# One layout, planner and schedule change in a planned fp32 kernel: operands at one remainder modulo 512 bytes, w2 sums off the operand ring

## The chip, the cores and the metric

One NeuronCore of a Trainium2 chip runs one launch. The metric is device time in microseconds, the median of repeated runs. In the profile, PE is TensorE's matmuls, PEld its weight loads, DVE VectorE, ACT ScalarE, POOL GpSimd, and SP SyncE, which issues every DMA.

## The reference

```python
xn = layernorm(x)                       # x: 2048 x 512, all float32
# A: linear attention, 32 heads of 16
q, k, v = split(xn @ wqkv)              # wqkv: 512 x 1536
pq, pk = phi(q), phi(k)                 # phi(t) = where(t > 0, t + 1, exp(t)) + 1e-6
o = (pq @ (pk.T @ v)) / (pq . sum(pk) + 1e-6)      # per head
A = o @ wo                              # wo: 512 x 512
# B: MLP, F = 1376
B = relu(xn @ w1 + b1) ** 2 @ w2 + b2
out = x + A + B
```

## The kernel before

**Arithmetic.** Products are made to nearly full fp32 precision from `float32r` parts: each operand is split into a rounded high part and the rest (`split`: a copy on ACT, a subtraction on DVE), and each product takes three matmuls of 128 x 512 (high x high, high x rest, rest x high).

**Stages.** Tokens go in tiles of 128. First all tiles are normalised, transposed (tiles 0 to 7 on TensorE, the rest by DVE behind small DMAs that regroup partitions, `xg<-xp`), projected on the k weights `wk`, and summed into `kx` (`acc<-pk,tok`). Then the four blocks of 512 tokens are handled in two pairs (`for n in range(2)`). A pair has a first phase, where each of NK = 7 pairs of column blocks (NQ = 2 of q, NP = 5 of w1) goes through seven half-size products (a Strassen-Winograd scheme on weights and on tokens, the sums of tokens being T1 to T4), and a second phase, `run_jobs`, where 21 jobs (first pair) or more multiply the activations `s` with rows of w2 or of the attention matrix. In the first pair the second phase is plain; in the second pair it uses the Strassen scheme again and so needs sums of blocks of w2.

**Operands.** Weights are split once, in the first pair, into tiles `ops` of two operands (512 KB), used and copied to DRAM (`spill`, into `wd1`, `wd2`, `wdz`), and later read back (`ops<-wd`). Eight slots D0 to D7 form a ring: `advance` hands a free slot to the next entry of the list `needed`, `used` frees a slot when its operands' matmuls are recorded. The w2 sums (`make_t`, from `raw_t` tiles in the slots x0 and x1) are entries of that list with no keys, two behind each of five steps of the second pair's first phase: they take a ring slot, are made by two additions and a split, and are spilled from it. The parts `s` of the activations rotate through five slots `pair0` to `pair4`.

**Order.** All instructions are recorded as tasks with their predecessors. TensorE's order is that of the code. Up to `nc.fixed` (the first tiles) all engines keep it; beyond, `Program.order` plays the program with costs for each instruction (`cost`), gives each task a due time from TensorE's order, and lets each engine, SP's DMA queue too, take the most urgent ready task, in 60 rounds in which waits of TensorE make the tasks before them more urgent (`press`); the best round is emitted. A new tile of a tag (`Place`) waits for the tasks recorded so far of the last tile there.

**Layout.** A tile gets its address when it is first used in the emitted order, behind those before it in its pool. The low pool holds, in the program as built and in bytes per partition: from address 1152 zb 512, ident 512, eps 64, b1s 64; then tiles of 8192 (B0, A0, xs1 high and rest, A1), four `pair` slots of 4096, less_one 64, the fifth `pair` slot, B1 (8192), the slots D and xs0 (both parts 8192), and zc 64. T1 to T4 lie in B0, B1, A0, A1, `wk` in A0 and A1. Small tiles are padded to 64 bytes. The rest, the raw tiles and `hz` among it, lies in a pool above.

**The second phases.** In the first pair the jobs are four attention products, `add_product(NK - 1, 1)` and the `hz` product, then for the second block four attention products, ten of w2 and the `hz` product; two jobs ahead, `parts_of` splits the next `s`. In the second pair `add_product(NK - 1, 1)` stands behind four of the five jobs of the first group.

Of the kernel before, what the change touches and what calls it, by code (L numbers as in the profile page):

```python
# [7 lines left out]
F32 = mybir.dt.float32  # L8
# [10 lines left out]
class Task:  # L19
    __slots__ = ("engine", "name", "args", "kw", "preds", "succs", "dur", "lag", "lock", "due", "ready", "left", "start", "at",  # L20
                 "index", "size", "cause", "behind")


class Place:
# [6 lines left out]
    def real(self):  # L31
        if self.tile is None:
            n = 1
            for k in self.shape[1:]:
                n *= k
            if n % 16 and self.pool.name.startswith("low"):
                t = self.pool.tile([self.shape[0], n + -n % 16], self.dt, name=self.name, tag=self.tag)[:, :n]
                if len(self.shape) > 2:
                    t = t.rearrange("p (a b) -> p a b", a=self.shape[1])
                self.tile = t  # L40
            else:
                self.tile = self.pool.tile(self.shape, self.dt, name=self.name, tag=self.tag)
        return self.tile
# [39 lines left out]
class Program:  # L83
# [29 lines left out]
    def add(self, engine, name, args, kw):  # L113
        t = Task()
        t.engine, t.name, t.args, t.kw, t.index = engine, name, args, kw, len(self.tasks)
        given = [("out" if k == 0 else "in", a) for k, a in enumerate(args)] + [("out" if k == "out" else "in", a) for k, a in kw.items()]
        given = [(k, a) for k, a in given if isinstance(a, (bass.AP, View))]
        outs, ins = ([self.region(a) for k, a in given if k == kind] for kind in ("out", "in"))
        if name == "matmul" and not kw.get("start"):
            ins = ins + outs  # L120
        outs = [r for r in outs if r[0] != self.apart]
        t.preds = {}
        for regions, write in ((ins, False), (outs, True)):
            for r in regions:
                before = self.seen.get(r[0], [])
                hit = [(o, wrote) for q, o, wrote in before
                       if (write or wrote) and q[0] < r[2] and r[1] < q[1] and q[2] < r[4] and r[3] < q[3]]
                if isinstance(r[0], Place) and r[0].last and not hit:
                    hit = [(o, True) for o in r[0].last.tasks]
                for o, wrote in hit:  # L130
                    if o is not t:
                        t.preds[o.index] = max(t.preds.get(o.index, 0), 1 if wrote else 0)
        for regions, write in ((outs, True), (ins, False)):
            for r in regions:
                old = self.seen.get(r[0], [])
                if write:
                    old = [x for x in old if not (x[1] is not t and r[1] <= x[0][0] and x[0][1] <= r[2] and r[3] <= x[0][2] and x[0][3] <= r[4])]
                self.seen[r[0]] = old + [(r[1:], t, write)]
                if isinstance(r[0], Place) and t not in r[0].tasks[-1:]:
                    r[0].tasks.append(t)  # L140
        self.cost(t, [a for k, a in given if k == "out"][0], [a for k, a in given if k == "in"])
        self.tasks.append(t)

    def cost(self, t, out, ins):
# [10 lines left out]
        if t.engine == "tensor":  # L155
            wide = t.name == "matmul" and ins[0].dtype != F32
            t.dur, t.lag = (0.0135 + n / 2400 if wide else 0.055 + n / 2400), 0.23
        elif t.engine == "scalar":
# [6 lines left out]
        elif t.engine == "gpsimd":  # L165
            t.dur = 0.2 + src * 2.3 / 1000 if t.name == "tensor_tensor" else 0.3
            t.lock = t.name == "tensor_tensor"
        else:
            b = 1
            for s, k in out.ap:  # L170
                b *= k
            run = 1
            for a in (out, *ins):
                d = list(a.ap)
                c = d[-1][1] if d[-1][0] == 1 else 1
                run = min(run, c) if run > 1 else c
            t.size, t.lag = 4 * b, 2.0
            t.dur = 0.43 if out.ap[0][1] == P and run >= 512 else 0.62
            t.size = t.size * max(1.0, (0.009 + run * 4 / 27e3) / (run * 4 / 24e3)) if run > 1 else b * 150
# [4 lines left out]
    def order(self):  # L184
# [3 lines left out]
        for t in ts:  # L188
            t.succs = []
        for t in ts:  # L190
            for p, raw in t.preds.items():
                ts[p].succs.append((t, raw))
        when = 0.0
        for t in ts:
            t.due = 1e9
            if t.engine == "tensor":
                t.due = when
                when += t.dur
        for t in reversed(ts):
            e = t.engine  # L200
            took = t.dur if e != "sync" else 2.0 + t.size / 380e3
            for s, raw in t.succs:
                t.due = min(t.due, s.due - took - (t.lag if raw and s.engine != e else 0))
            t.due = min(t.due, when)
# [26 lines left out]
    def play(self):  # L231
# [18 lines left out]
        while done < len(ts):  # L250
# [27 lines left out]
            if e == "sync":  # L278
                dma = end = max(dma, end) + t.size / 380e3
            done += 1  # L280
# [24 lines left out]
def kernel(  # L305
# [10 lines left out]
):  # L316

# [108 lines left out]

    def both(name, tags, dt=F32R, pool=keep):
# [9 lines left out]
    NK = NQ + NP  # L456
    wd1 = [dram.tile([P, 7, 512], F32, name=f"wd1_{k}") for k in range(NK)]
    wd2 = [dram.tile([P, 8, 512], F32, name=f"wd2_{k}") for k in range(NK)]
    wdz = dram.tile([P, 4, 512], F32, name="wdz")
    wdm = [dram.tile([P, 512], F32, name=f"wdm_{j}") for j in range(NJ)]  # L460
    wos = {}
    ident = keep.tile([P, P], F32, name="ident")
    heads = work.tile([P, P], F32, name="heads", tag="heads")
    b1s = keep.tile([P, NF], F32, name="b1s")
    zb = keep.tile([P, P], F32, name="zb")
    zc = keep.tile([P, 2, NJ], F32, name="zc")
    eps = keep.tile([P, 1], F32, name="eps")

# [59 lines left out]
    def spill(kind, k, i, t):  # L528
        n = t.shape[1]
        nc.sync.dma_start(place_of(kind, k, slice(i, i + n)), f32(t))  # L530
        ready.update((kind, k, i + e) for e in range(n))
# [244 lines left out]

    def place_of(kind, k, i):
        return wdz[:, i] if kind == "z" else (wd1 if kind == "1" else wd2)[k][:, i]

    def load_keys(keys):  # L780

        def make(t):
            (kind, k, i), two_of = keys[0], len(keys) == 2
            if two_of and keys[1] == (kind, k, i + 1):
                nc.sync.dma_start(f32(t), place_of(kind, k, slice(i, i + 2)))
            else:
                for e, key in enumerate(keys):
                    nc.sync.dma_start(f32(t[:, e]), place_of(*key))
        return make

    def advance():

        while needed and free_ops:
# [8 lines left out]
            for e, key in enumerate(keys):  # L802
                loaded.setdefault(key, []).append((t[:, e], holder))
            if not keys:
                free_ops.append(tag)

# [14 lines left out]
    def needed_in(n):  # L821
# [6 lines left out]
        for p in range(NK + 1):  # L828
# [13 lines left out]
            if p < NK:  # L842
# [3 lines left out]
                if f >= 0 and n:  # L846
                    o.append(([("2", f, 2)], None))
                if n and 0 < p <= NP:
                    for e in range(2):
                        o.append(([], make_t(p - 1, e)))  # L850

        def attention(make):
            for j in range(NJ):
                both_of("2", NP + j // 2, 2 * (j % 2), make_2(NP + j // 2, j % 2) if make else None)

        if n == 0:
            attention(True)
            both_of("2", NP - 1, 2, make_2(NP - 1, 1))
            both_of("z", 0, 2, make_z(1))
# [6 lines left out]

        keys = [("2", f, 4) for f in range(NP - 1)] + [("2", NP - 1, 2), ("2", NP - 1, 4)]

# [320 lines left out]

    less_one = keep.tile([P, 1], F32, name="less_one")  # L1190
    nc.gpsimd.memset(less_one, -1.0)
# [80 lines left out]
    for n in range(2):  # L1272
# [19 lines left out]

        if n:
            raw_free[:] = ["x0", "x1"]
            raw_jobs += [raw_2(k, "t") for k in range(NP)]
            fetch_raws()
        banks = [bank(f"b{n}_{k}", loop_tag) for k in range(4)]
# [127 lines left out]
        if n == 0:  # L1425
            jobs = [attention_job(acc, 0, j) for j in range(NJ)]
            jobs.append((None, lambda s: add_product(NK - 1, 1)))
            jobs.append(z_job(acc, 0, True))
# [7 lines left out]
            outs.append(lambda: store(res[t1], t1, 0, 1))  # L1436

            def step(e):
                if e == 10:
# [3 lines left out]
                if e > 1:  # L1443
                    do(columns if columns else sums)

            later_jobs = [attention_job(acc_2, 2, j, j == 0) for j in range(NJ)]
# [8 lines left out]
            def prepare(job):  # L1455
                if job[0] is None:
                    return None
                if len(job) == 3:
                    square(job[0])
                return parts_of("s", job[0])  # L1460

            run_jobs([(j[0], j[1]) if len(j) == 2 else (j[0], True, j[1]) for j in jobs + later_jobs],
                     lambda j: prepare(j), 2, step)
            do(outs, len(outs))
            do(columns, len(columns))
# [40 lines left out]

        jobs.insert(NP - 1, (None, lambda s: add_product(NK - 1, 1)))
        o = {}
# [48 lines left out]
```

## Time and profile before

| | |
|---|---|
| median of 3 runs | 440.11 us (439.18 to 440.42) |
| the profiled execution | 439.19 us, span 437.5 us |
| granted clock of TensorE | 0.988 (mean) |
| PE, DVE, ACT busy in the span | 416.8, 325.7, 256.0 us |
| DMA | 96.19 MB, 220 GB/s on average |
| the chain that ended last | PE 84%, DMA 9%, DVE 3% of the span |

PE rows of the timeline give a start and a modelled length: the length of a row runs past the start of the next, so the pace is read from the starts. All instructions come from one recording helper, so their line is always L293 and groups are told apart by tile names.

### The profile page before, as it was taken

What the parts mean: (1) busy time and instruction counts of PE and PEld (TensorE: products, weight loads), DVE (VectorE), ACT (ScalarE), POOL (GpSimd) and SP (SyncE); (2) the same over time, 40 slices, a digit from 0 to 9 for tenths busy, and PEclk for the clock granted to TensorE, in tenths of its full rate; (3) what the DMA queues carried; (4) which work ended last, traced back from release to release, by engine and by line L of the source; (5) the groups of instructions that cost most, each with busy time, mean ns of one, the idle gap of its engine ahead of it and who ended that gap; (6) DMA issues with size and microseconds to landing.
All of it is one profiled execution on the core that took longest, in us unless ns stands there. A gap on an engine that the chain in (4) does not pass through costs nothing.

```text
span 437.5 us, 5497 instructions
## 1 busy us (share of the span) xinstructions
PE 416.8 (95%) x1808; PEld 335.3 (77%) x1808; DVE 325.7 (74%) x551; ACT 256.0 (59%) x438; POOL 27.4 (6%) x48
## 2 busy tenths in 40 slices
PE   8999859999999999999999999999898999999993
PEld 7788648888888888888878888888676887788882
DVE  5899578888868898999919720998787985466953
ACT  5775355664957888888814220568676784435310
POOL 2242122220000000000000000000000000000000
PEclk9999969999999999999999999999999999999998
DMA  7850753921897669754967997798788889958703
GB/s 237 279 152 1 193 168 96 273 65 49 288 327 285 254 235 326 264 214 181 326 250 181 248 347 258 208 306 264 279 248 279 254 253 233 287 160 230 196 0 97
DMA packets 78273, 96.19 MB, mean 220 GB/s; under 512 B 40003, under 2 KB 51267, under 8 KB 77989
## 3 DMA queue, kind: packets, MB, share of 16 engines
q1 hardware_dynamic: 78244, 95.84, 70.1%
q8 instruction: 14, 0.23, 0.2%
q14 instruction: 15, 0.11, 0.1%
HBM read 59.91 MB, written 33.82 MB: 214 GB/s over the span
## 4 chain that ended last, share of the span: by engine, by line
PE 84%; DMA 9%; DVE 3%; SPq 1%; ACT 1%; issue 0%; POOL 0%; POOLq 0%
PE ps L293 48%; PE acc L293 36%; DMA wd<-ops 4%; DMA ops<-wd 2%; DMA xTd<-t 1%; SPq L293 1%; DMA x<-in_A_x_dram 1%; DVE y L293 1%; DMA xg<-xp 0%; DVE xp L293 0%; DVE ops L293 0%; DVE st L293 0%; DVE res L293 0%; DVE o L293 0%; ACT s L293 0%
## 5 line engine op out<-in xcount | busy, mean ns | idle before, releaser
L293 PE MATMUL ps<-s,ops 128*128 128x512 f32 x390 | 95.2, 394 | 0.0
L293 PEld LDWEIGHTS ps<-s,ops 128*128 128x128 f32 x390 | 72.8, 187 | 18.1 <-ACT s L293 0.6
L293 PE MATMUL acc<-s,ops 128*128 128x512 f32 x300 | 74.5, 394 | 2.2 <-ACT s L293 1.4
L293 PEld LDWEIGHTS acc<-s,ops 128*128 128x128 f32 x300 | 55.9, 187 | 16.9 <-ACT s L293 2.3
L293 PE MATMUL acc<-pk,tok 128*128 128x512 f32 x192 | 47.6, 396 | 0.0
L293 ACT ACTIVATE s<-rr 128x512 fp32r<-128x512 f32 x46 | 28.5, 629 | 26.0 <-PE acc L293 13.8
L293 DVE TENSOR_TENSOR s<-rr,s 128x512 fp32r<-128x512 f32 x46 | 31.4, 687 | 16.4 <-ACT s L293 15.3
L293 PE MATMUL ps<-T,ops 128*128 128x512 f32 x168 | 42.4, 394 | 0.0
L293 PEld LDWEIGHTS acc<-pk,tok 128*128 128x128 f32 x192 | 35.7, 189 | 8.4 <-DVE pk L293 0.6
L293 PE MATMUL acc<-T,ops 128*128 128x512 f32 x168 | 42.1, 394 | 0.0
L293 PEld LDWEIGHTS acc<-T,ops 128*128 128x128 f32 x168 | 31.5, 187 | 7.5
L293 PEld LDWEIGHTS ps<-T,ops 128*128 128x128 f32 x168 | 31.4, 187 | 7.4
L293 ACT ACTIVATE rr<-acc 128x512 f32<-128x512 f32 x23 | 13.5, 587 | 20.3 <-PE acc L293 20.1
L293 POOL TENSOR_TENSOR tok<-xp,tok 128x512 fp32r<-128x512 f32 x16 | 22.2, 1390 | 43.4 <-ACT tok L293 38.6
L293 PE MATMUL ps<-xs0h,ops 128*128 128x512 f32 x72 | 23.8, 391 | 0.0
L293 PE MATMUL acc<-xs0h,ops 128*128 128x512 f32 x56 | 18.6, 393 | 3.3 <-DMA ops<-wd 3.3
L293 ACT ACTIVATE ops<-raw 128x512 fp32r<-128x512 f32 (+1 forms) x28 | 16.3, 590 | 7.4 <-DMA raw<-in_B_w_dram 3.2
L293 DVE TENSOR_TENSOR ops<-raw,ops 128x512 fp32r<-128x512 f32 (+1 forms) x28 | 17.0, 618 | 3.5 <-ACT ops L293 3.5
L293 PE MATMUL ps<-wkh,xs1h 128*128 128x512 f32 x32 | 13.5, 433 | 6.3 <-ACT xs1h L293 6.2
L293 DVE TENSOR_TENSOR rr<-acc,rr 128x512 f32<-128x512 f32 x21 | 14.4, 688 | 5.6 <-PE acc L293 4.7
L293 ACT ACTIVATE k<-ps 128x512 f32<-128x512 f32 x16 | 9.5, 594 | 15.2 <-PE ps L293 15.0
L293 ACT ACTIVATE tok<-xp 128x512 fp32r<-128x512 f32 x16 | 10.0, 625 | 10.6 <-POOL xp L293 8.8
(153 smaller groups left out, 735.8 us busy)
## 6 DMA issues: line engine op xcount, KB each, us to landing
wd<-ops SPq DMA_DIRECT2D x45, 512.0 KB, 5.1
ops<-wd SPq DMA_DIRECT2D x43, 512.0 KB, 5.5
ops<-wd SPq DMA_DIRECT2D x42, 256.0 KB, 4.5
res<-in_A_x_dram SPq DMA_DIRECT2D x32, 128.0 KB, 5.3
out_dram<-res SPq DMA_DIRECT2D x32, 128.0 KB, 4.3
x<-in_A_x_dram SPq DMA_DIRECT2D x5, 512.0 KB, 6.3
raw<-in_B_w_dram SPq DMA_DIRECT2D x10, 256.0 KB, 6.5
raw<-in_B_w_dram SPq DMA_DIRECT2D x5, 512.0 KB, 4.7
```

The source lines that it names most:

```text
L293: getattr(getattr(self.nc, t.engine), t.name)(*map(real, t.args), **{k: real(a) for k, a in t.kw.items()})
```

## The change

- `eps`, `b1s`, `zc` and `less_one` become slices of one tile `odds` of 256 bytes; the padding to 64 bytes goes.
- `add` notes the last tile of a place (`first`) and `order` binds a new tile to all its tasks, also those recorded later; due times are worked out in topological order. Costs: matmuls of plain fp32 dearer, DMAs above 64 KB with 2.8 us to land instead of 2.0, 320 GB/s instead of 380.
- `wd1`, `wd2`, `wdz` are laid out by pairs of operands: `[4, P, 2, 512]` instead of `[P, 7 or 8, 512]`.
- The w2 sums leave `needed`: they are made in the first pair's second phase, from the fifth job on, in the slots rp0 and rp1, two a job, once all raw slots are free; spilled from there.
- `add_product(NK - 1, 1)` comes one job earlier in both second phases, and its operand with it in the lists of keys.

```diff
-                    hit = [(o, True) for o in r[0].last.tasks]
+                    t.first.append(r[0].last)
...
-            t.dur, t.lag = (0.0135 + n / 2400 if wide else 0.055 + n / 2400), 0.23
+            t.dur, t.lag = (0.0135 + n / 2400 if wide else 0.055 + n / 2400 if t.name == "transpose" else 0.11 + n / 1200), 0.23
...
-            t.size, t.lag = 4 * b, 2.0
+            t.size, t.lag = 4 * b, 2.8 if b > P * P else 2.0
...
+            for place in t.first:
+                for o in place.tasks:
+                    t.preds.setdefault(o.index, 1)
...
-            took = t.dur if e != "sync" else 2.0 + t.size / 380e3
+            took = t.dur if e != "sync" else t.lag + t.size / 320e3
...
-                dma = end = max(dma, end) + t.size / 380e3
+                dma = end = max(dma, end) + t.size / 320e3
...
-    wd1 = [dram.tile([P, 7, 512], F32, name=f"wd1_{k}") for k in range(NK)]
-    wd2 = [dram.tile([P, 8, 512], F32, name=f"wd2_{k}") for k in range(NK)]
-    wdz = dram.tile([P, 4, 512], F32, name="wdz")
+    wd1 = [dram.tile([4, P, 2, 512], F32, name=f"wd1_{k}") for k in range(NK)]
+    wd2 = [dram.tile([4, P, 2, 512], F32, name=f"wd2_{k}") for k in range(NK)]
+    wdz = dram.tile([2, P, 2, 512], F32, name="wdz")
...
-    b1s = keep.tile([P, NF], F32, name="b1s")
+    odds = keep.tile([P, P // 2], F32, name="odds")
+    b1s, zc = odds[:, 16:16 + NF], odds[:, 32:32 + 2 * NJ].rearrange("p (u j) -> p u j", u=2)
-    zc = keep.tile([P, 2, NJ], F32, name="zc")
-    eps = keep.tile([P, 1], F32, name="eps")
+    eps = odds[:, :1]
...
-                if n and 0 < p <= NP:
-                    for e in range(2):
-                        o.append(([], make_t(p - 1, e)))
...
             for j in range(NJ):
+                if make and j == NJ - 1:
+                    both_of("2", NP - 1, 2, make_2(NP - 1, 1))
                 both_of("2", NP + j // 2, 2 * (j % 2), make_2(NP + j // 2, j % 2) if make else None)
...
-        keys = [("2", f, 4) for f in range(NP - 1)] + [("2", NP - 1, 2), ("2", NP - 1, 4)]
+        keys = [("2", f, 4) for f in range(NP)]
+        keys.insert(NP - 2, ("2", NP - 1, 2))
...
-    less_one = keep.tile([P, 1], F32, name="less_one")
+    less_one = odds[:, 1:2]
...
-        if n:
-            raw_free[:] = ["x0", "x1"]
-            raw_jobs += [raw_2(k, "t") for k in range(NP)]
-            fetch_raws()
...
-            jobs.append((None, lambda s: add_product(NK - 1, 1)))
+            jobs.insert(NJ - 1, (None, lambda s: add_product(NK - 1, 1)))
...
+                if e > 3:
+                    if not made_t and sorted(raw_free) == ["rp0", "rp1", "x0", "x1"]:
+                        raw_free[:] = ["x0", "x1"]
+                        raw_jobs.extend(raw_2(k, "t") for k in range(NP))
+                        fetch_raws()
+                    if len(raw_free) < 4:
+                        for u in range(2 * (len(made_t) < NP)):
+                            make_t(len(made_t), u)(work.tile([P, 2, 512], F32R, name="made", tag=f"rp{u}"))
+                        made_t.append(e)
...
-        jobs.insert(NP - 1, (None, lambda s: add_product(NK - 1, 1)))
+        jobs.insert(NP - 2, (None, lambda s: add_product(NK - 1, 1)))
```

More of the change, by code (lines that the diff above doesn't have):

```diff
@@ L20 @@
     __slots__ = ("engine", "name", "args", "kw", "preds", "succs", "dur", "lag", "lock", "due", "ready", "left", "start", "at",
-                 "index", "size", "cause", "behind")
+                 "index", "size", "cause", "behind", "first")
 class Place:
@@ L32, in real @@
         if self.tile is None:
[L33 to L42, printed above, removed]
+            self.tile = self.pool.tile(self.shape, self.dt, name=self.name, tag=self.tag)
         return self.tile
@@ L121, in add @@
         outs = [r for r in outs if r[0] != self.apart]
-        t.preds = {}
+        t.preds, t.first = {}, []
         for regions, write in ((ins, False), (outs, True)):
@@ L190, in order @@
         for t in ts:
+            for place in t.first:
+                for o in place.tasks:
+                    t.preds.setdefault(o.index, 1)
+            t.left = len(t.preds)
+        for t in ts:
             for p, raw in t.preds.items():
                 ts[p].succs.append((t, raw))
+        line = [t for t in ts if not t.left]
+        for t in line:
+            for s, raw in t.succs:
+                s.left -= 1
+                if not s.left:
+                    line.append(s)
         when = 0.0
@@ L198, in order @@
                 when += t.dur
-        for t in reversed(ts):
+        for t in reversed(line):
             e = t.engine
-            took = t.dur if e != "sync" else 2.0 + t.size / 380e3
+            took = t.dur if e != "sync" else t.lag + t.size / 320e3
             for s, raw in t.succs:
@@ L529, in spill @@
         n = t.shape[1]
-        nc.sync.dma_start(place_of(kind, k, slice(i, i + n)), f32(t))
+        nc.sync.dma_start(place_of(kind, k, i, n), f32(t))
         ready.update((kind, k, i + e) for e in range(n))
@@ L775, with place_of @@
     ready, loaded, owner, needed, free_ops = set(), {}, [], [], []
-    def place_of(kind, k, i):
-        return wdz[:, i] if kind == "z" else (wd1 if kind == "1" else wd2)[k][:, i]
+    def place_of(kind, k, i, n=1):
+        at = slice(i % 2, i % 2 + n)
+        return (wdz if kind == "z" else (wd1 if kind == "1" else wd2)[k])[i // 2, :, at]
     def load_keys(keys):
@@ L784, in make @@
             if two_of and keys[1] == (kind, k, i + 1):
-                nc.sync.dma_start(f32(t), place_of(kind, k, slice(i, i + 2)))
+                nc.sync.dma_start(f32(t), place_of(kind, k, i, 2))
             else:
                 for e, key in enumerate(keys):
-                    nc.sync.dma_start(f32(t[:, e]), place_of(*key))
+                    nc.sync.dma_start(f32(t[:, e:e + 1]), place_of(*key))
         return make
@@ L803, in advance @@
                 loaded.setdefault(key, []).append((t[:, e], holder))
-            if not keys:
-                free_ops.append(tag)
     def op(*key):
@@ L857, in needed_in @@
             attention(True)
-            both_of("2", NP - 1, 2, make_2(NP - 1, 1))
             both_of("z", 0, 2, make_z(1))
@@ L1436 @@
             outs.append(lambda: store(res[t1], t1, 0, 1))
+            made_t = []
             def step(e):
@@ L1463 @@
                      lambda j: prepare(j), 2, step)
+            assert len(made_t) >= NP, made_t
             do(outs, len(outs))
```

## The prediction

> **What bounds the kernel now.** I read the page first, then the stages, then who ended TensorE's waits, and last the start times of single matmuls.
>
> ```profile
> span 437.5 us, 5497 instructions
> PE 416.8 (95%) x1808; PEld 335.3 (77%) x1808; DVE 325.7 (74%) x551; ACT 256.0 (59%) x438; POOL 27.4 (6%) x48
> GB/s 237 279 152 1 193 168 96 273 65 49 288 327 285 254 235 326 264 214 181 326 250 181 248 347 258 208 306 264 279 248 279 254 253 233 287 160 230 196 0 97
> ```
>
> TensorE is busy 95% of the span, so time can come from two places alone: the 20.7 us in which it is idle, and the pace of its matmuls. The stages from 59 us on (projections, first pair's first and second phase, second pair's first and second phase with the tail) give the idle part.
>
> ```profile
> 59.00:107.00 48.00, 47.55 (x195) 38.63 (x196) 41.45 (x59) 30.01 (x50) 10.58 (x12) 0.94 0.47 136
> 107.00:215.00 108.00, 108.00 (x484) 88.01 (x484) 94.53 (x161) 88.15 (x147) 0.52 (x1) 1.00 0.74 261
> 215.00:275.00 60.00, 59.28 (x256) 47.46 (x255) 27.97 (x40) 15.29 (x24) 0.00 (x0) 1.00 0.84 257
> 275.00:365.00 90.00, 85.94 (x369) 68.28 (x368) 77.80 (x133) 64.94 (x106) 0.00 (x0) 1.00 0.87 265
> 365.00:437.50 72.50, 64.60 (x276) 51.33 (x276) 40.40 (x62) 23.14 (x39) 0.00 (x0) 0.97 0.60 167
> ```
>
> The columns are the length, the busy time of PE, PEld, DVE, ACT and POOL, the granted clock, the DMA share and GB/s. From 107 us on TensorE lacks 0.7 us in the first pair's second phase and 4.1 us in the second pair's first phase. The tail's idle time is outside the change. The waits by who ended them:
>
> ```profile
> PE ps L293 <- ACT xs1h L293: 6.2, 1, 6.2
> PE acc L293 <- DMA ops<-wd: 3.3, 2, 1.9
> PE acc L293 <- ACT s L293: 1.4, 2, 0.7
> PE acc L293 <- ACT rr L293: 0.8, 1, 0.8
> ```
>
> 3.3 us are operand loads that came late, 1.4 us are two waits for a moving operand `s`, 0.8 us is the last relu of the second pair, and 6.2 us lie in the start. Now the pace. In the timeline of TensorE, the distance between two rows' starts over the number of matmuls is the pace:
>
> ```profile
> 70.42 2.88 PE L293 MATMUL acc<-pk,tok 128*128 128x512 f32 x12
> 73.14 0.39 PE L293 MATMUL ps<-wkh,xs1h 128*128 128x512 f32 x1
> ...
> 321.88 0.39 PE L293 MATMUL acc<-xs0h,ops 128*128 128x512 f32 x1
> ...
> 324.62 1.56 PE L293 MATMUL acc<-T,ops 128*128 128x512 f32 x6
> 326.02 1.54 PE L293 MATMUL ps<-s,ops 128*128 128x512 f32 x6
> 327.40 0.86 PE L293 MATMUL acc<-T,ops 128*128 128x512 f32 x3
> ```
>
> Equal matmuls run at two paces: `acc<-pk,tok` 2.72/12 = 226.7 ns, `xs0` against `ops` (321.88 to 324.62) 2.74/12 = 228.3 ns, `T` against `ops` 1.40/6 = 233.3 ns, and this `s` 1.38/6 = 230 ns. What tells them apart is where the tiles lie. Adding up the tile sizes in order of first use (the layout above), `ops` and `xs0` start at 320 modulo 512 bytes; `xs1`, T1, T3, T4 and four of the five `pair` slots at 256; T2 and the fifth slot at 320. `pk` and `tok` at 70 us are both at 256. So equal remainders of the moving tile and the weights go with 226.7 ns, after a few irregular matmuls behind each switch (hence 228.3), and a 64-byte difference with 233.3. A long stretch agrees:
>
> ```profile
> 232.07 41.82 PE ps L293 x180
> ```
>
> 41.82/180 = 232.3 ns, which is four fifths of 233.3 and one fifth of 228.3: the mixture of pair slots.
>
> **The change part by part.** *Operands equal modulo 512.* In the new layout only zb and ident (512 bytes each) and `odds` (256) stand ahead of the operands, and all else there is a multiple of 4096: every operand of the low pool gets the same remainder. The groups that leave the slow pace:
>
> ```profile
> L293 PE MATMUL ps<-s,ops 128*128 128x512 f32 x390 | 95.2, 394 | 0.0
> L293 PE MATMUL acc<-s,ops 128*128 128x512 f32 x300 | 74.5, 394 | 2.2 <-ACT s L293 1.4 <-ACT rr L293 0.8
> L293 PE MATMUL ps<-T,ops 128*128 128x512 f32 x168 | 42.4, 394 | 0.0
> L293 PE MATMUL acc<-T,ops 128*128 128x512 f32 x168 | 42.1, 394 | 0.0
> L293 PE MATMUL ps<-xs1h,ops 128*128 128x512 f32 x44 | 15.3, 394 | 0.0
> L293 PE MATMUL acc<-xs1h,ops 128*128 128x512 f32 x28 | 9.9, 394 | 0.0
> L293 PE MATMUL ps<-xs1l,ops 128*128 128x512 f32 x22 | 8.7, 394 | 0.0
> L293 PE MATMUL acc<-xs1l,ops 128*128 128x512 f32 x14 | 5.5, 394 | 0.0
> ```
>
> (390 + 300) x 4/5 + (168 + 168) x 3/4 + 108 = 912 matmuls by 6.67 ns = 6.1 us. The other 138 + 84 of `s` and `T`, some 18 runs of 12, no longer settle anew: 18 x 0.02 = 0.4 us. Sum -6.5 us. The bounds are 0, if the remainders are not the cause, and -7.8 if each of the 195 matmuls of the second stage gained 6.67 ns as well. I take -6.5, since the two paces stand side by side in the rows. It counts in full only while TensorE stays the bound: in the first phase of the first pair DVE works 94.5 of 108 us, and after this step of some 105; in the second pair's 77.8 of 90. Neither becomes the longer one.
>
> By the Trainium skill, "SBUF — State Buffer", section "SBUF: two separate sides", only the port pair that VectorE and GpSimd share causes contention and TensorE never waits on anyone, so addresses could not matter. The two paces of equal matmuls side by side do not agree with that; it is a rival below.
>
> *The sums leave the operand ring.* In the second pair's first phase the ring of eight also carries ten tiles of w2 sums, each holding its slot until its copy to DRAM has landed. The chain of waits passes there:
>
> ```profile
> 297.92 6.67 DMA wd<-ops
> 304.65 4.35 DMA ops<-wd
> 309.14 4.38 PE acc L293 x18
> ```
>
> A copy of 6.67 us frees a slot, the load into it takes 4.35, and TensorE starts 1.9 us late; the second such wait brings it to 3.3. Without these tiles in the ring no load stands behind a copy, and eight slots are ahead of TensorE. -3.3 us; bounds 0 and -3.3. What is late next there is DVE, which loses work as well.
>
> The moved work: eight of the ten sum pairs run after 275 us now (DVE busy, count, clock, DMA share, GB/s of the additions alone):
>
> ```profile
> 231.00:253.00 22.00, 1.60 (x4) 1.00 0.94 232
> 253.00:275.00 22.00, 0.00 (x0) 1.00 0.83 283
> 275.00:297.00 22.00, 2.46 (x6) 1.00 0.92 279
> 297.00:319.00 22.00, 2.35 (x6) 1.00 0.81 263
> 319.00:341.00 22.00, 1.59 (x4) 1.00 0.83 269
> ```
>
> Each is two additions of 0.4 us (6.4 us for sixteen), a rounding copy on ACT and a subtraction on DVE:
>
> ```profile
> 295.36 0.68 ACT L293 ACTIVATE ops<-t 128x512 fp32r<-128x512 f32 x1
> 296.79 0.68 DVE L293 TENSOR_TENSOR ops<-t,ops 128x512 fp32r<-128x512 f32 x1
> ```
>
> So 6.4 + 8 x 0.68 = 11.8 us of DVE and 5.4 us of ACT enter the stage from 215 to 275, where DVE is busy 28 of 60 us and ACT 15: nothing on the path, taken at 0; without that cover it would be 11.8 us. Their DMAs go past SP's queue: at most ten copies and five loads of 512 KB, 7.9 MB. The added waits are those of the copies for DVE; behind them in SP's order stand the operand loads of TensorE. Bounds 0 and the price of the second rival; I take 0, as these bytes are wanted only in the last phase and the loads have eight slots of 12 matmuls (2.75 us each) in hand.
>
> *The product moved one job ahead.* Both waits for `s` have one pattern:
>
> ```profile
> 228.32 0.63 ACT L293 ACTIVATE s<-hz 128x512 fp32r<-128x512 f32 x1 [9.56 <-PE acc L293]
> 229.01 3.06 PE L293 MATMUL acc<-s,ops 128*128 128x512 f32 x12 [0.72 <-ACT s L293]
> ...
> 372.85 1.67 PE L293 MATMUL acc<-s,ops 128*128 128x512 f32 x6 [0.72 <-ACT s L293]
> ```
>
> `add_product(NK - 1, 1)` still uses its pair slot when the job after it, five pairs on, wants the slot: ACT starts when the product ends, TensorE waits 0.72 us. One job earlier, 12 matmuls (6 in the second pair) lie between, 2.7 or 1.4 us against the 0.72 needed. -1.4 us; bounds 0 and -1.4. Its own operand is wanted a job earlier too, which the key lists follow.
>
> *DRAM by operand* changes addresses and no sizes. No row shows the new form; the loads stay eight slots ahead, so 0, and with that cover gone a few tenths either way. *The planner* (late uses, dearer plain fp32 matmuls, slower DMA) keeps TensorE's order but may reorder DVE, ACT, POOL and SP everywhere; no row shows the new order. It could at best take the 6.2 us wait of the start and what the lower clock behind it costs (0.06 of 48 us, 2.9 us), and at worst add a wait of that size: -9.1 to +9.1. I take 0: the edits touch no step of that chain.
>
> Sum: -6.5 - 3.3 - 1.4 = -11.2 us. The profiled execution took 439.19 us, 1.7 of them outside the span, giving 428.0; the median of the runs is 440.11, 0.9 above it, so 428.9.
>
> **The rivals.** *The pace is not set by addresses* (the rule above): only the waits go, 4.7 us, 435.4. Against it: the match at 232.07. For it: only these remainders were seen, not the new one (384). *The first pair's second phase becomes DMA-bound, slower than before.* From 231 to 275 DMA moves (232 + 283) x 22 = 11.3 MB. With 7.9 MB more it has 19.2 MB, and if SP puts them ahead of operand loads, at 283 GB/s that takes 68 us instead of 44: +24 against -11.2, 452.9. It decides from 11.2 us, that is 19.2 MB in 55.2 us, 348 GB/s, about the page's best slice (347). Against it: some of the loads are there already, and nothing asks for the copies before the last phase, so most may flow past 275 us, where the same bytes vanish. Milder, it costs 2 to 6 us. *The plan does not follow*: the sums are off the ring, but the new order opens a wait in the start as large as the present one: +6.2, 435.1. *The plan closes the start's wait*: -9.1, 419.8.
>
> **How the numbers follow.** Forecast as summed 0.68, itself 424 to 433; pace unchanged 0.10; DMA-bound 0.11, half of it beyond the old time; a new wait 0.06; a better start 0.05. 0.3% of 440 us is 1.3 us, about what can be told from no change. Faster 0.90: all but the worse half of the second rival and the tails of the first and third; same 0.03, slower 0.07. The range from 421.5 to 436 takes in the first and third rival and the mild second, and leaves out some 0.15.
>
> **What would show it.** Right: chain rows of 12 matmuls at 2.72 us in all phases and `PE ps x180` near 40.8; no `PE acc <- DMA ops<-wd` row; no 0.72 waits on `ACT s`; additions on `raw_t` all before about 280 us. Wrong: 2.80 rows remaining (pace), `DMA ops<-wd` waits between 215 and 275 us (second rival), a wait on `xs1h` over 6.2 us (third).

## The result and the profile after

The changed kernel takes 415.74 us (median of 4 runs, 415.53 to 416.01); the kernel before 439.64 us (4 runs, 437.17 to 440.42). The ratio is 0.9466 [0.9427, 0.9505], 23.9 us less. The forecast was 428.9 us, its range 421.5 to 436.0: the direction was right, the gain more than twice as large as the 11.2 us forecast.

The page after, its span, the engines and the chain of work that ended last:

```profile
span 414.0 us, 5503 instructions
PE 404.5 (98%) x1808; PEld 334.2 (81%) x1808; DVE 326.8 (79%) x551; ACT 256.4 (62%) x438; POOL 27.8 (7%) x48
PE 96%; DVE 2%; DMA 1%; ACT 0%; issue 0%
```

TensorE was idle for 20.7 us of its span and is idle for 9.5 now; it is also busy 12.3 us less (416.8 to 404.5), with the same 1808 matmuls. The chain is TensorE's almost alone (96%, before 84%): after the first microseconds no DMA stands on it. The stages of the changed kernel (length, busy time of PE, PEld, DVE, ACT and POOL, granted clock, DMA share, GB/s), cut at the same times as before:

```profile
0.00:59.00 59.00, 57.30 (x264) 47.18 (x265) 50.73 (x116) 40.16 (x85) 17.92 (x37) 1.00 0.60 180
59.00:107.00 48.00, 48.00 (x214) 39.74 (x213) 43.10 (x58) 31.33 (x53) 9.33 (x10) 1.00 0.58 175
...
215.00:275.00 60.00, 60.00 (x266) 49.71 (x265) 35.94 (x62) 19.29 (x32) 0.00 (x0) 1.00 0.98 303
275.00:365.00 90.00, 89.22 (x393) 73.32 (x393) 67.47 (x110) 61.88 (x103) 0.00 (x0) 1.00 0.83 244
```

In the second row 214 matmuls are done where it was 195, at a clock of 1.00 where it was 0.94: the start, where the forecast expected nothing, has changed. The 0.94 was a mean. In the kernel before, the clock granted behind the wait on `xs1h` was 0.50 up to 65 us and 1.00 from there:

```profile
59.00:65.00 6.00, 5.55 (x13) 4.39 (x14) 5.89 (x13) 3.61 (x8) 2.02 (x2) 0.50 0.62 208
65.00:107.00 42.00, 42.00 (x183) 34.24 (x183) 35.55 (x47) 26.40 (x43) 8.55 (x10) 1.00 0.45 126
```

What TensorE of the changed kernel still waits for, by who ended the wait:

```profile
PE ps L295 <- DVE odds L295: 1.1, 1, 1.1
PE acc L295 <- ACT rr L295: 0.8, 1, 0.8
PE acc L295 <- DVE xp L295: 0.3, 1, 0.3
PE acc L295 <- DVE y L295: 0.3, 1, 0.3
```

The rows for `xs1h` (6.2 us), for operands from DRAM (3.3 us) and for `s` (1.4 us) are all gone. The pace, in the chain of waits:

```profile
47.01 2.72 PE ps L295 x12
49.73 2.72 PE acc L295 x12
...
218.09 40.80 PE ps L295 x180
```

40.80/180 = 226.7 ns, where the same 180 took 41.82 us.

**Where the 23.5 us of span went.** TensorE's order is that of the code in both kernels, so the start of the n-th matmul in one trace can be set against the n-th in the other. The changed kernel gets ahead by 0.6 us up to 44 us; by 9.3 us between 44 and 65 us of the time before, nearly all of it the wait on `xs1h` (6.4 from start to start, of which 6.2 idle) and the slow matmuls behind it (2.7); by 3.8 us at the two waits for operands and by 2.0 us at the two waits for `s`, each counted from the matmul before the wait to the fourth behind it; and by 7.6 us spread over all other stretches from 65 us on (0.7 up to 107 us, 2.0 up to 215 us, 4.9 after), which is the pace. The last 0.2 us lie behind the last matmul. The 0.6 us of the first 44 are mostly pace too: in the run below that has the new layout alone, the same matmuls are 0.5 us ahead of the kernel before. The forecast had the waits for operands, those for `s` and the pace; the 9.3 us are what it missed.

The missed piece can be read in SyncE's queue. The timeline of its DMA issues in the kernel before (start, length, target and source, count):

```profile
43.06 0.37 SPq L293 DMA_DIRECT2D wv<-in_A_wqkv_dram  x1
43.52 0.52 SPq L293 DMA_DIRECT2D xTd<-t  x1
44.09 12.04 SPq L293 DMA_DIRECT2D xg<-xp  x16
```

its longest wait there (us in total, times, longest):

```profile
SPq L293 <- DVE xp L293: 13.1, 1, 13.1
```

and the same queue in the changed kernel:

```profile
35.35 10.09 SPq L295 DMA_DIRECT2D xg<-xp  x16
45.54 0.57 SPq L295 DMA_DIRECT2D xTd<-t  x1
46.22 1.25 SPq L295 DMA_DIRECT2D wv<-in_A_wqkv_dram  x1
```

The load of `wv` goes into the place of raw tokens (tiles 4 to 7), so it may only start when the last of them has been normalised. These normalisations are recorded behind the first use of `wv`'s place, so the old planner didn't count them: it took the load for ready and put it ahead of the 16 small DMAs `xg<-xp` that regroup tile 8. The queue is worked in order; SyncE stood 13.1 us before the load, and the regrouping of the tile that gives `xs1` waited behind it without need. Now the 16 stand ahead and begin 8.7 us earlier.

### The profile page after: what moved, and what is told of

Same layout as the page of the kernel before. It is cut to its first block, busy times and chain, and to the rows that moved or that the text cites. A ratio compares the mean times of both kernels' runs of the same rounds, so it can differ in the third digit from the quotient of the medians.

```text
span 414.0 us, 5503 instructions
## 1 busy us (share of the span) xinstructions
PE 404.5 (98%) x1808; PEld 334.2 (81%) x1808; DVE 326.8 (79%) x551; ACT 256.4 (62%) x438; POOL 27.8 (7%) x48
## 4 chain that ended last, share of the span: by engine, by line
PE 96%; DVE 2%; DMA 1%; ACT 0%; issue 0%
PE ps L295 51%; PE acc L295 45%; DMA x<-in_A_x_dram 1%; DVE res L295 0%; DVE o L295 0%; DVE st L295 0%; DVE xp L295 0%; DVE y L295 0%; ACT rr L295 0%; DVE mv L295 0%
## 5 line engine op out<-in xcount | busy, mean ns | idle before, releaser
L295 PE MATMUL ps<-s,ops 128*128 128x512 f32 x390 | 92.9, 389 | 0.0
L295 PE MATMUL acc<-s,ops 128*128 128x512 f32 x300 | 72.7, 390 | 0.8 <-ACT rr L295 0.8
L295 PEld LDWEIGHTS acc<-s,ops 128*128 128x128 f32 x300 | 56.2, 188 | 13.1 <-ACT rr L295 1.2
L295 PE MATMUL ps<-T,ops 128*128 128x512 f32 x168 | 41.4, 390 | 0.0
L295 PE MATMUL acc<-T,ops 128*128 128x512 f32 x168 | 41.2, 389 | 0.0
L295 DVE TENSOR_TENSOR ops<-raw,ops 128x512 fp32r<-128x512 f32 (+1 forms) x28 | 18.7, 676 | 1.5 <-ACT ops L295 1.3
L295 ACT ACTIVATE s<-rf 128x512 fp32r<-128x512 f32 x10 | 6.3, 633 | 18.0 <-PE ps L295 17.6
L295 ACT ACTIVATE rr<-rr,odds 128x512 f32<-128x512 f32 x15 | 10.8, 723 | 9.2 <-DVE rr L295 9.1
```

What stands on the lines that cost most here:

```text
L295: getattr(getattr(self.nc, t.engine), t.name)(*map(real, t.args), **{k: real(a) for k, a in t.kw.items()})
```

## The experiments

**One part at a time, on the kernel before.** First the late uses, counted for the one place `wv`:

```diff
...
-                    hit = [(o, True) for o in r[0].last.tasks]
+                    if r[0].name == "wv":
+                        t.first.append(r[0].last)
+                    else:
+                        hit = [(o, True) for o in r[0].last.tasks]
...
```

> The kernel before, with the late uses counted for one place alone, the tile wv of the v weights. Theory (head of line): in the kernel before, the planner believes that the load of wv may start early, because the last readers of the tile that lies there (the normalisations of tokens 4 to 7) are recorded after wv; in truth SP waits for them 13.1 us and the 16 regrouping DMAs of tile 8 stand behind it. With the uses counted the load is put behind these DMAs: the wait on xs1h of 6.2 us and the low clock after it are gone, 439.6 - 9.3 = 430.3 us. Rival (costs): the new DMA and matmul costs of the planner closed the wait; then 439.6 us and the wait of 6.2 us stays.

Measured 429.88 us against 438.71, ratio 0.9797 [0.9768, 0.9826]. Its waits of TensorE:

```profile
PE acc L307 <- DMA ops<-wd: 3.1, 2, 1.7
PE acc L307 <- ACT s L307: 1.4, 2, 0.7
PE ps L307 <- DVE eps L307: 1.1, 1, 1.1
```

No row for `xs1h` is left, the others are those of before, and the 16 `xg<-xp` begin at 37.41 us with the load of `wv` behind them. One load put in the right place of a queue is worth 8.8 us: the missed piece, alone.

Then the layout: `odds` in place of the small tiles, no padding, all else as before.

> The kernel before with the tile odds alone: every operand at 384 modulo 512 bytes, all instructions in the same order. Theory (equal remainders): rows of 12 matmuls take 2.72 us in all phases; 7.0 to 7.5 us less, 432.4 us, with the 6.2 us wait of the start and the late operand loads still there. Rival (addresses do not matter): 439.6 us, PE ps x180 at 41.8 us.

431.71 us, ratio 0.9834 [0.9813, 0.9855], 7.0 us less; the wait on `xs1h` (6.6 us) and that for operands (3.1 us) stay. The 180 matmuls that took 41.82 us take

```profile
227.52 40.80 PE ps L284 x180
```

So addresses alone, with the same instructions in the same order, are worth about what the forecast gave the pace.

The product and its operand one job ahead:

> The kernel before with add_product(NK - 1, 1) one job earlier in both second phases, and its operand with it. Theory (pair slot): the two waits of 0.72 us on ACT s go, with the irregular matmuls behind them 1.8 to 2.0 us, 437.7 us. Rival: the wait comes back elsewhere (on the operand or on the next s), 439.6 us.

436.74 us, ratio 0.9950 [0.9935, 0.9965]: 2.0 us less. Both waits on `s` are gone and the other long waits are as before.

The w2 sums off the ring and into the first pair's second phase:

> The kernel before with the w2 sums made in the first pair's second phase off the operand ring, nothing else. Theory (ring): the two waits of together 3.3 us for ops<-wd in the second pair's first phase go, 3.3 to 3.9 us less, 436.0 us; DVE takes the sums in the stage from 215 to 275 us without a wait of TensorE. Rival (DMA-bound): the copies and loads make operand loads late between 215 and 275 us, waits of 2 us or more there, 438 us or above.

A miss: 455.71 us, ratio 1.0385 [1.0355, 1.0415], 17 us slower. Its waits:

```profile
PE ps L293 <- DMA ops<-wd: 15.8, 3, 14.7
PE acc L293 <- DVE pk L293: 7.8, 1, 7.8
```

The two waits in the second pair went as expected, but at 258 us TensorE began a wait of 14.7 us for an operand, in the phase that the sums were moved into. The second row is the start's wait, which here ends on another tile. Late operands in that phase are what the forecast's second rival had said, and only the rest of the change can have kept them away. Two guesses followed: the planner's dearer DMAs, and the late uses.

> The kernel before with the w2 sums off the ring and the planner's new costs. Made because the sums alone were 17 us slower: TensorE waited 14.7 us for an operand load at 258 us, behind which SP's queue held copies of the tiles made that waited for DVE again and again. Theory (DMA price): with 2.0 us to land the planner took the round trip of a slot rp0 or rp1 (copy out, next sum) for shorter than the 5 to 6 us it takes and issued copies ahead of urgent loads; with 2.8 us and 320 GB/s the wait of 14.7 us is gone and that of 6.2 us in the start stays: 436 us. Rival (late uses): the wait stays, 450 us or more.

455.82 us, ratio 1.0367 [1.0328, 1.0405]: the theory of the prices fell, with the same longest wait of 14.7 us.

> The kernel before with the w2 sums off the ring and all late uses counted, with the old costs. Theory (DMA price): the start's wait goes (9.3 us less), but operand loads are late between 230 and 290 us as with the sums alone: 440 to 446 us. Rival (late uses closed both): no wait in that stage, 426 us.

440.69 us, ratio 1.002 [0.9993, 1.0047]. This lies within what the fallen theory had expected and far above the 426 of its rival. The start's wait is gone, which by the first run is worth 8.8 us, but between 225 and 290 us stand 5.6 us on `s` and 4.5 us on operands. The late uses change the harm and don't end it. Of what is left, the layout of the copies in DRAM is the suspect. In the program, what an access in DRAM touches is one range of addresses:

```python
        reach = sum((n - 1) * s for s, n in dims[1:]) + 1
...
        if not in_psum(a):
            reach += (dims[0][1] - 1) * dims[0][0]
            return a.tensor.name, 0, 1, a.offset, a.offset + reach
```

In a tile `[P, 8, 512]` a pair of operands is strided over all partitions, so its range takes in nearly all of the tile, and the load of one pair counts as dependent on the copy of another that was recorded earlier. Recorded in the first pair's second phase, the copies of the sums come ahead of loads of the same `wd2` tiles; in `[4, P, 2, 512]` each pair has a range of its own.

**The DRAM layout, added and taken away.** Sums off the ring plus the DRAM copies by operand, on the kernel before:

> The kernel before with the w2 sums off the ring and the DRAM copies by operand; planner, layout and job order as before. Theory (false order through DRAM: in tiles of [P, 8, 512] the program takes a copy of one operand and a load of another of the same tile to touch the same range, so the loads of the first pair's second phase are queued on SP behind copies of sums that DVE has yet to make; a place of its own for each pair of operands ends that): the late operand loads that the sums alone brought (14.7 us of waits on `ops` between 215 and 290 us) are gone, the two ring waits (3.3 us) are gone too, the start's wait on `xs1h` (6.2 to 6.6 us) stays; 440.1 - 3.3 - 1 = 435 to 437 us. Rival (the moved copies crowd the DMA engines whatever their layout): 450 us or more, with the waits of the run of the sums alone.

437.53 us, ratio 0.9941 [0.9919, 0.9962], 18 us less than the sums alone. Its waits:

```profile
PE ps L293 <- ACT xs1h L293: 6.4, 1, 6.4
PE acc L293 <- ACT rr L293: 3.6, 3, 1.4
PE acc L293 <- ACT s L293: 1.4, 2, 0.7
```

No operand comes late any more, in either phase. The gain is 2.7 us and not 3.3 or more, since two new waits of 1.4 us opened in the second pair, each for a relu to empty the PSUM bank that TensorE is to sum into next. And the other way round, the changed kernel with the old DRAM tiles:

```diff
...
-    wd2 = [dram.tile([4, P, 2, 512], F32, name=f"wd2_{k}") for k in range(NK)]
+    wd2 = [dram.tile([P, 8, 512], F32, name=f"wd2_{k}") for k in range(NK)]
...
```

> The changed kernel with the DRAM copies back in the old tiles of 7 and 8 operands; everything else as changed. Theory (false order through DRAM): waits of TensorE on DMA-loaded `ops` between 215 and 290 us come back; the run of sums with late uses had 4 to 10 us of them and of what follows, the sums alone 14.7: 422 to 431 us, 426 the likeliest. Rival (the layout of the copies does not matter, the late uses and the job order made the sums harmless): 415.7 us.

437.98 us (434.95 to 438.34; ratio 0.9946 [0.9922, 0.9970]): 22.2 us more than the changed kernel, the theory's side by far, though above the range that it had given. The chain of waits of its profiled execution (span 433.2 us):

```profile
219.29 21.77 PE ps L295 x96
242.36 0.70 DVE made L295
243.08 5.85 DMA wd<-made
249.72 0.70 DVE made L295
250.81 4.29 DMA ops<-wd
255.23 5.46 PE ps L295 x12
260.83 3.16 PE ps L295 x12
264.37 5.24 DMA ops<-wd
269.75 8.43 PE ps L295 x36
```

Here the order is to be seen: a sum is made by DVE, its copy takes 5.85 us, the next is made and its copy issued, and only then is the load that TensorE wants issued. TensorE idles for 11.5 and 3.1 us, and between the two 12 matmuls take 5.46 us instead of 2.72, at a granted clock of 0.50 between 255 and 261 us. It is the order and not the volume: in this stage the run moved less than the changed kernel did.

```profile
215.00:275.00 60.00, 45.35 (x186) 36.24 (x186) 29.58 (x46) 14.20 (x22) 0.00 (x0) 0.89 0.89 272
```

272 GB/s, against 303 in the changed kernel, where no operand was late. Nor are single transfers slower in the old tiles. The loads of 512 KB take, from issue to landing (median, first in this run, then in the changed kernel):

```profile
ops<-wd SPq DMA_DIRECT2D x43, 512.0 KB, 4.6
ops<-wd SPq DMA_DIRECT2D x43, 512.0 KB, 5.3
```

That the overlapping ranges make this order is read from the program; that the DRAM tiles are its cause is shown by these two runs, since each differs in nothing else from the one it is compared with.

**The rest of the change, taken away from the changed kernel.** Late uses not counted for `wv` alone:

> The kernel after without the late uses of the one place wv. Theory (head of line): the wait of 6.2 us before tile 8 and the low clock behind it come back, 415.7 + 9.3 = 425.0 us; the rest as after. Rival (costs): 415.7 us.

426.23 us, ratio to before 0.969 [0.9656, 0.9724]: 10.5 us more. The wait comes back at 50 us on another tile (`pk`), behind the old order in SyncE's queue (`wv` at 42.67 us, the 16 `xg<-xp` from 43.71 us on):

```profile
PE acc L298 <- DVE pk L298: 8.0, 1, 8.0
```

The planner's old prices:

> The changed kernel with the planner's old prices (plain fp32 matmuls at the fast price, DMA 2.0 us and 380 GB/s); late uses, layout, sums, DRAM copies and job order as changed. Theory (the start's wait is a matter of order, which the late uses alone set right): no wait on `xs1h`, 415.7 us within 1.5. Rival (the new prices are needed to time the start): a wait of 3 to 7 us between 45 and 65 us, 419 to 425 us.

417.08 us, ratio 0.9484 [0.9461, 0.9506], 1.3 us more. The start is as good as in the changed kernel: the prices are not needed for it. But a wait of 1.8 us for a bank opens at 266 us:

```profile
PE acc L295 <- ACT rr L295: 2.6, 2, 1.8
```

**The addresses by themselves.** The changed kernel with 64 unused bytes ahead of the ring of operands, so that `ops` lies at 448 and all other operands at 384 modulo 512:

```diff
+            if self.tag[0] == "D" and not hasattr(Place, "pad"):
+                Place.pad = self.pool.tile([P, 64 // 4], F32, name="pad", tag="pad")
```

> The kernel after with 64 unused bytes ahead of the operand slots: same instructions in the same order, ops at 448 and all moving tiles at 384 modulo 512. Theory (equal remainders): matmuls on ops go back to 233.3 ns, those of the projections and of pk with tok stay at 226.7; some 1370 matmuls by 6.67 ns = 9 us more, 424.8 us. Rival (addresses do not matter): 415.7 us.

424.55 us, ratio 0.9653 [0.9622, 0.9685], 8.8 us more than the changed kernel. The long stretch of its chain:

```profile
221.48 42.00 PE ps L297 x180
```

42.00/180 = 233.3 ns. 1326 matmuls read `ops`, and 1326 by 6.67 ns is 8.8 us. All engines have the same instructions in the same order, so the address is the cause. That it is the address against that of the moving tile, and not that of `ops` alone, the kernel before shows: by the layout its `ops` lie at 320, and they go at 226.7 ns with `xs0` (320, once settled) and at 233.3 with T (256).

**A version that beats both.** In the second pair's second phase the first job of one group waited 0.8 us for the last relu to empty its PSUM bank. The two pairs of banks exchanged:

```diff
-        Y, W = ([bank(f"{u}{c}", loop_tag) for c in range(2)] for u in "YW")
+        W, Y = ([bank(f"{u}{c}", loop_tag) for c in range(2)] for u in "WY")
```

> The changed kernel with the two pairs of PSUM banks of the last phase exchanged (groups W and Y), so that the first attention job of group Y does not wait for the last relu to empty its bank. Theory: the 0.8 us wait of `acc` on ACT `rr` near 343 us goes, and nothing else moves: 414.9 us. Rival (another wait, of group W for the same banks, takes its place): 415.7 us or a little more.

414.83 us (5 runs, 414.75 to 414.90; the changed kernel, measured earlier, 415.53 to 416.01), ratio to before 0.943 [0.941, 0.9449]. The wait on `rr` is gone and none took its place.

## Why the prediction was wrong

**The pace** was right in cause and nearly in size: -6.5 forecast, 7.6 us in the trace from 65 us on, 7.0 alone. The second stage, which it left for the bound of -7.8, brought 0.7 us of this. The -6.5 had left out a slow group of the projections: by the forecast's own layout `wk` lies at 256 and `xs0` at 320, and in the kernel before 12 matmuls of the two take 2.80 us (47.50 to 50.30), 233.3 ns each. The rival that addresses don't matter is out by the run with 64 bytes more. So is, for this kernel, the rule of the Trainium skill, "SBUF — State Buffer", section "SBUF: two separate sides", that TensorE never waits on anyone, if it is read as saying that its operands' addresses are free: 233.3 against 226.7 ns. No run tells where the 6.67 ns are lost.

**The ring** (-3.3) came to 3.8 us and **the product** (-1.4) to 2.0, in the trace as alone: the idle time as forecast, and behind each of the four waits some irregular matmuls that the forecast didn't count.

**The planner** is the step that failed. The prediction gave it -9.1 to +9.1 and wrote "I take 0: the edits touch no step of that chain." They do: the step is the load of `wv` at the head of SyncE's queue. The forecast had priced the start's wait rightly (6.2 us and 2.9 for the clock; the trace gives 6.4 and 2.7), and the rule that a new tile waits for tasks "recorded so far" stood ahead of it; but it shows no row of that wait's chain and doesn't ask what orders SyncE. The row that gives it, a wait of 13.1 us, stands in the view of the waits of SyncE's own queue, and the forecast makes no use of it. With it, the rival "the plan closes the start's wait" would have been the better forecast: 419.8 us instead of 428.9. Of the 4.1 us from there to 415.74 the terms above give 1.1, 0.5 and 0.6; the first 65 us brought 0.8 more than 9.1, most of it pace, and the end 0.2. The forecast stood on a median 0.9 us above the execution that it was worked out from, and the changed kernel's median is close to its own profiled execution.

**DRAM by operand** at 0 is the second wrong step, hidden in the total, since here it came with the sums. "Changes addresses and no sizes" is true and beside the point: the addresses set what the planner takes for dependent. Together with the sums it is worth 18 us (455.71 to 437.53), taken from the change 22.2. Alone, without the sums, it wasn't run.

**The moved sums** at 0 held in the changed kernel: DVE is busy 35.9 of 60 us in that stage. The additions on `raw_t` end at 283 us, about as forecast. But the cover was not the eight slots that the forecast had in hand: without the DRAM edit those slots ran empty. The second rival had the right place and sign for the sums alone, and its condition, that SP puts other transfers ahead of the operand loads, is what happened. Its price was wrong in kind: it counted more bytes than the DMA engines could move in time (the point was 348 GB/s), and what held up the loads was the order of a queue, at 272 GB/s.

The parts run alone sum to 8.8 + 7.0 + 2.0 + 2.7 = 20.5 us of the 23.9. What makes up the other 3.4 us is not shown. The new prices are worth 1.3 us in the changed kernel, the late use of `wv` 10.5 there against 8.8 alone, and the waits for banks that opened beside the sums are absent there; the combinations were not run.

## What to carry to other kernels

Where one queue issues all transfers, read who that queue itself waits for: a transfer that can't start yet holds up all behind it, and the engine that idles names quite another tile. When a planner's rules change, ask of each long wait whether an instruction ahead of it in its queue was put there by a dependence missed (`wv`) or by one that isn't real (the DRAM ranges). An edit "of addresses only" can be both an instruction's pace and a queue's order. An edit that moves work into idle time should be judged with the edit that keeps its transfers out of the way, and each should also be tried alone.

## What the runs showed of the hardware that was not expected

Equal matmuls of 128x128 by 128x512 in fp32r go at 226.7 ns one after the other where the moving tile and the weights have the same remainder modulo 512 bytes (pairs at 256 and at 320 in the kernel before, at 384 in the changed one), and at 233.3 ns where `ops` lies 64 bytes further in the partition: 2.9%, over 1326 matmuls 8.8 us. The remainders come from adding up tile sizes, and the only difference tried is 64 bytes: whether 512 is the period, and what other differences cost, no run here tells.

A long idle gap cost more than its length. Behind the 6.2 us wait at 53 us TensorE lost 2.7 us more, at a granted clock of 0.50 from 59 to 65 us; behind the gap of 11.5 us in the run with the old DRAM tiles, 12 matmuls took 5.46 us instead of 2.72, at 0.50 as well. The two waits of 1.9 and 1.3 us in the second pair's first phase left the clock of their stage at 1.00.
